# TensorE in program order after the first ninth, and a strided head's second products laid out with the summands adjacent

## The chip, the cores and the metric

One Trainium2 chip, one core, one launch. The metric is the device time of the execution in microseconds (us), the median of the runs shown. Profiles are of one profiled execution each.

## The reference, cut to what matters

Inputs: `q`, `k`, `v` of 8 samples x 8 heads x 576 positions x 64, and the weights `U` (576 x 32), `V` (32 x 576), `w_ch1` (512 x 2048), `w_ch2` (2048 x 512).

```python
scores = q @ k.T / 8                                  # per sample and head, 576 x 576
mask_local   = (rel >= 0) & (rel < 32)                # heads 0 to 3, rel = i - j
mask_strided = (rel >= 0) & (j % 32 == i % 32)        # heads 4 to 7
attn = softmax(where(mask, scores, -1e9)) ; x = attn @ v      # x: 8 x 576 x 512
u  = x + (x.T @ U @ V).T                              # mix along the positions, rank 32
ch = relu(u @ w_ch1) @ w_ch2
out = u + ch
```

## The kernel before, in words

**The large products.** The 8 x 576 = 4608 rows of `u` are worked off in nine blocks of 512 columns (`n` = 0 to 8; here: ninths 0 to 8). Eight of them are the first 512 positions of a sample; the last ninth is the 64 remaining positions of all eight. A ninth has 16 slices `fc` of the 2048 hidden features. `gemm1(n, fc)` (L598) makes one slice in PSUM (`ph`, two buffers) with 12 matmuls of 128x128 by 128x512; ScalarE makes `gh` (Relu) from it, VectorE `gl`, the remainder of the rounding, in `gemm1_out` (L615). `gemm2(n, fc)` (L625) adds that slice to the four accumulators with 12 more matmuls. `gemm2` lags two slices behind (`LAG`). The two `acc` tiles take the whole pool, so the first `gemm2` of a ninth needs the accumulators that `finish` (L656) of the ninth before empties: VectorE adds `ul`, GpSimd adds `uh`, a DMA stores `o`.

**The loop and its ticks.** In the loop over `n` at L916 each slice is cut into four pieces of 6 matmuls, and after each piece comes a `tick` (L814): 64 ticks in a ninth, each with 6 large matmuls. A tick takes one step of each task that is due. While ninth `n` is multiplied, `plan(n)` (L800) brings sample `b = n + 1` to its `u`: `pairs` (the four local heads as two pairs, `attention_pair`, L318, staggered by `run_staggered`, L667), `mix0` and `mix1` (`mix_t`, L462: x times U for the local and for the strided half), `u0` and `u1` (`u_local`, L512; `u_strided`, L528; `u_tail`, L578: times V, plus x, split into two parts). The number after the name is the first tick, a name in brackets the task that must have been written before.

**The strided heads.** `strided_heads(b)` (L348) works the four strided heads of a sample without TensorE: a residue class of 18 positions per partition, `st0` holding q and later the result, `st1` holding k and then v. GpSimd multiplies q by 9 keys at a time into `tmp` (L366), VectorE adds over the 64 dimensions into `s_st`; softmax; then GpSimd multiplies the 18 weights of a row by v into `tmp` (L392; 27 products a sample, of 64 to 576 elements a partition), and VectorE adds over the positions `j` into `st0`. In `tmp` the order is (j, d), so that VectorE reads with a step of 64 or 32 elements. VectorE then transposes the result into `xS`, and ScalarE copies it into `x_str`, which `mix1` reads. In all 74 calls of the generator, at 1.3 a tick (1.45 for the first sample that takes this way). They begin in the last ticks of the ninth before (`EARLY`, L933).

**What sets the order.** `InOrder` (L59) ties each instruction of an engine to the one traced before it, as long as the class's `on` is true. It is switched off for all engines at the end of ninth 0 (L912). From then on the framework's scheduler orders each engine's queue by a timeline of its own, with the traced order as priority. Each engine then works its queue strictly in that order: an instruction that waits holds up everything behind it. The same holds for the DMA queue of SyncE.

**The small products of TensorE** (`px`) share one PSUM tile: one may begin only when the readers of the one before are through. `mix_steps` (L422) takes four partial sums over U in PSUM, copies the first into SBUF (`ta`) and adds the other three there with VectorE. `ta` lies in unused rows of `x_loc` or `x_str` (rows 64 to 95 of the last slot).

The pool `att` has seven buffers for everything short-lived: kT, qT, s_sb, blocks, PT, tmp, xT, xS, tl and o.

Of the kernel before, what the change touches and what calls it, by code (L numbers as in the profile page):

```python
# [14 lines left out]
ALU = mybir.AluOpType  # L15
AX = mybir.AxisListType
# [8 lines left out]
NB = B * S // TB  # L25
NSP = 2
LAG = 2
EARLY = 56


ATT_BUFS = 7
# [16 lines left out]
def fused_kernel(ctx, tc, lqk, lv, eqk, ev, sqkv, U, V, wts, masks, eye, out):  # L48
# [10 lines left out]
    class InOrder:  # L59
# [5 lines left out]
        def __getattr__(self, name):  # L65
            op = getattr(self.engine, name)

            def call(*args, **kwargs):
                with tc.issue_after(self.last) if InOrder.on and self.last is not None else nullcontext():
                    r = op(*args, **kwargs)  # L70
                self.last = r.ins
                return r

            return call
# [243 lines left out]
    def attention_pair(b, pr, loaded=None):  # L318
        if loaded is None:
            loaded = pair_loads(b, pr)  # L320
            for _ in range(3):
                yield
        kT, qT, vt = loaded
        sp = masked(kT, qT)
        yield
        s_sb = masked_shifted(sp, masks_sb[:, 0:320])
        yield
        exponentials(s_sb)
        yield
        yield  # L330
        turned(s_sb.rearrange("p t h (e x) -> p t (h e) x", x=32), p_store[pr])
        yield
        yield
        PT = fetched(p_store[pr], "PT")
        for _ in range(6 + 9 * pr):
            yield
        op = outputs(PT, vt, lambda c: 160 * (c % 4) + 32 * (c // 4))
        yield
        normalised(op, pr)
        yield  # L340
        turned(x_loc[:, :, 128 * pr:128 * pr + 128].rearrange("p t (e x) -> p t e x", x=32), x_store[pr])
        yield

    o_str = {}

    def strided_heads(b):  # L348
        st = [ap_.tile([128, NCH * D], F32, name=f"st{x}") for x in range(2)]
        sq, sk = (z.rearrange("p (i d) -> p i d", d=D) for z in st)  # L350
        for x in range(2):
            dma(out=st[x], in_=sqkv[b - NSP, x])
        yield
        s_st = ap_.tile([128, NCH, NCH], F32, name="s_st")
        nc.gpsimd.memset(s_st, 8.0 * NEG)
        late = []

        def flush(n):
            while len(late) > n:
                late.pop(0)()  # L360

        for i in range(NCH):
            for j0 in range(0, i + 1, 9):
                n = min(9, i + 1 - j0)
                tmp = att([128, 9, D], "tmp")
                nc.gpsimd.tensor_tensor(out=tmp[:, 0:n], in0=sk[:, j0:j0 + n], in1=sq[:, i:i + 1].broadcast_to([128, n, D]),  # L366
                                        op=ALU.mult)
                late.append(lambda tmp=tmp, n=n, i=i, j0=j0: vector.tensor_reduce(
                    out=s_st[:, i, j0:j0 + n], in_=tmp[:, 0:n], axis=AX.X, op=ALU.add))
                flush(1)  # L370
                yield
        flush(0)
        sv = sk
        dma(out=st[1], in_=sqkv[b - NSP, 2])
        yield
        m_st = ap_.tile([128, NCH], F32, name="m_st")
        vector.tensor_reduce(out=m_st, in_=s_st, axis=AX.X, op=ALU.max)
        vector.tensor_tensor(out=s_st, in0=s_st, in1=m_st.broadcast_to([128, NCH, NCH]), op=ALU.subtract)
        scalar.activation(out=s_st, in_=s_st, func=AF.Exp, scale=0.125)
        yield  # L380
        yield
        vector.tensor_reduce(out=m_st, in_=s_st, axis=AX.X, op=ALU.add)
        vector.tensor_scalar(out=m_st, in0=m_st, scalar1=1e-9, scalar2=None, op0=ALU.add)
        vector.reciprocal(out=m_st, in_=m_st)
        vector.tensor_tensor(out=s_st, in0=s_st, in1=m_st.broadcast_to([128, NCH, NCH]), op=ALU.mult)
        yield
        for i in range(NCH):
            step = D if i < 9 else D // 2
            for d0 in range(0, D, step):
                tmp = att([128, (i + 1) * step], "tmp")  # L390
                tv = tmp.rearrange("p (j d) -> p j d", d=step)
                nc.gpsimd.tensor_tensor(out=tv, in0=sv[:, 0:i + 1, d0:d0 + step],  # L392
                                        in1=s_st[:, i, 0:i + 1].broadcast_to([128, i + 1, step]), op=ALU.mult)
                late.append(lambda tv=tv, i=i, d0=d0, step=step: vector.tensor_reduce(
                    out=sq[:, i, d0:d0 + step], in_=tv.rearrange("p j d -> p d j"), axis=AX.X, op=ALU.add))
                flush(1)
                yield
        flush(0)
        yield
        o_str[b] = []  # L400
        for e in range(2):
            xT = att([128, S], "xS")
            vector.transpose(out=xT.rearrange("p (i r) -> p i r", r=32), in_=sq[:, :, 32 * e:32 * e + 32])
            o_str[b].append(xT)
        yield
        for h in range(4):
            rows = slice(32 * h, 32 * h + 32)
            xh = x_str.rearrange("p t (e h x) -> p t h e x", e=2, h=4)[:, :, h]
            oh = sq[rows].rearrange("p i (e x) -> p i e x", e=2)
            for i4 in range(4):  # L410
                scalar.copy(out=xh[32 * i4:32 * i4 + 32, 0:4], in_=oh[:, i4:16:4])
                if i4 % 2:
                    yield
            for i4 in range(2):
                scalar.copy(out=xh[32 * i4:32 * i4 + 32, 4], in_=oh[:, 16 + i4])
            yield
# [5 lines left out]
    def mix_steps(b, half):  # L422
        x, uv = (x_str, 1 if b < NSP else 0) if half else (x_loc, 0)
        ps_a = psx2()[:, 0, 0:256]
        for j in range(4):
            tensor.matmul(ps_a[32 * j:32 * j + 32, :], U_sb[:, uv, j, :], x[:, j, :], start=True, stop=False,
                             skip_group_check=True, tile_position=(0, 32 * j))
        for j in range(4):
            part = slice(64 * j, 64 * j + 64)
            tensor.matmul(ps_a[32 * j:32 * j + 32, part], U_sb[0:64, uv, 4, :], x[0:64, 4, part], start=False, stop=True,  # L430
                             skip_group_check=True, tile_position=(0, 32 * j))
        yield 1
        ta = x[64:96, 4, :]
        scalar.copy(out=ta, in_=ps_a[0:32, :])
        yield 1
        for j in range(1, 4):
            vector.tensor_tensor(out=ta, in0=ps_a[32 * j:32 * j + 32, :], in1=ta, op=ALU.add)
        if b not in tsts:
            tsts[b] = ap_.tile([96, DM], F32R, name="tst")
        yield 1  # L440
        dst = tsts[b][:, 256 * half:256 * half + 256]
        scalar.copy(out=dst[0:32], in_=ta)
        scalar.copy(out=dst[32:64], in_=ta)
        yield 1
        vector.tensor_tensor(out=dst[64:96], in0=ta, in1=dst[0:32].bitcast(F32), op=ALU.subtract)
# [16 lines left out]
    def mix_t(b, half):  # L462
        finished(mix_steps(b, half))
# [114 lines left out]
    def u_tail(b):  # L578
        finished(u_tail_steps(b))
# [87 lines left out]
    def run_staggered(gens, lag):  # L667
        live, waiting, n = [], list(gens), 0
        while live or waiting:
            if waiting and n % lag == 0:  # L670
                live.append(waiting.pop(0))
            n += 1
            for g in list(live):
                if next(g, "end") == "end":
                    live.remove(g)
            yield
# [115 lines left out]
    def task(gen, key, start, rate=1.0, after=()):  # L792
        return [gen, key, start, rate, after, 0.0]

    def calls(*fns):
        for fn in fns:
            fn()
            yield

    def plan(n):  # L800
        b = n + 1
        if b < B:
            return [
                task(run_staggered([attention_pair(b, 0), attention_pair(b, 1)], 8), "pairs", 0, 1.0),
                task(calls(lambda: mix_t(b, 0)), "mix0", 43, 1.0, ("pairs",)),
                task(u_local(b), "u0", 48, 1.0, ("mix0",)),
                task(calls(lambda: mix_t(b, 1)), "mix1", 51 if n == 1 else 49, 1.0, ("str",)),
                task(calls(lambda: u_strided(b), lambda: u_tail(b)), "u1", 54 if n == 1 else 56, 1.0, ("mix1", "u0")),
            ]
        if b == B:  # L810
            return [task(u_rest(), "rest", 12)]
        return []
# [67 lines left out]
    def first_block():  # L880
# [18 lines left out]
        while pieces or agenda:  # L899
# [9 lines left out]
                if delay:  # L909
                    agenda.append((now + delay, item[1], item[2]))  # L910
            clock["now"] += 1
        InOrder.on = False  # L912

    first_block()
    heads = None
# [111 lines left out]
```

## Time and profile before

| | |
|---|---|
| time, median of 3 runs (least to most) | 923.17 us (920.92 to 924.85) |
| the profiled execution | 923.34 us, span 921.6 us |
| TensorE busy | 889.6 us, 97% of the span |
| VectorE busy | 565.3 us, 61% |
| GpSimd busy | 383.4 us, 42% |
| ScalarE busy | 256.6 us, 28% |
| granted TensorE clock | 1.00 throughout |

How to read it: PE is TensorE (its matmuls), DVE VectorE, ACT ScalarE, POOL GpSimd, SP the engine that issues the DMAs. Almost every line is L70, the helper that issues an instruction, so groups are told apart by the tile written and the tiles read (`gl<-ph,gh`). A figure in square brackets is the idle time of the engine just before an instruction, and after the arrow what ended it.

### The profile page before, as it was taken

What the parts mean: (1) busy time and instruction counts of PE and PEld (TensorE: products, weight loads), DVE (VectorE), ACT (ScalarE), POOL (GpSimd) and SP (SyncE); (2) the same over time, 40 slices, a digit from 0 to 9 for tenths busy, and PEclk for the clock granted to TensorE, in tenths of its full rate; (3) what the DMA queues carried; (4) which work ended last, traced back from release to release, by engine and by line L of the source; (5) the groups of instructions that cost most, each with busy time, mean ns of one, the idle gap of its engine ahead of it and who ended that gap; (6) DMA issues with size and microseconds to landing.
All of it is one profiled execution on the core that took longest, in us unless ns stands there. A gap on an engine that the chain in (4) does not pass through costs nothing.

```text
span 921.6 us, 16237 instructions
## 1 busy us (share of the span) xinstructions
PE 889.6 (97%) x6622; PEld 706.0 (77%) x6622; DVE 565.3 (61%) x967; ACT 256.6 (28%) x514; POOL 383.4 (42%) x410
## 2 busy tenths in 40 slices
PE   7999999998999989999999899999999999999998
PEld 4677778876788678877887688867887888888886
DVE  5988875778587855696568756686569431112112
ACT  5866741105110521133112321052114311111110
POOL 1000024764876566475748466557646220002000
PEclk9999999999999999999999999999999999999999
DMA  9992112222143303321142304331331030001001
GB/s 292 405 405 98 53 58 68 77 89 87 32 127 96 99 26 106 96 96 53 48 127 62 109 13 127 96 97 32 101 96 46 1 98 0 1 1 46 1 0 47
DMA packets 46779, 80.95 MB, mean 88 GB/s; under 512 B 10896, under 2 KB 23952, under 8 KB 46704
## 3 DMA queue, kind: packets, MB, share of 16 engines
q1 hardware_dynamic: 46704, 79.91, 26.7%
q8 instruction: 52, 0.85, 0.4%
q14 instruction: 23, 0.19, 0.1%
HBM read 61.54 MB, written 18.35 MB: 87 GB/s over the span
## 4 chain that ended last, share of the span: by engine, by line
PE 45%; DVE 23%; DMA 14%; POOL 10%; issue 3%; SPq 3%; ACT 1%; POOLq 0%; DVEq 0%; ACTq 0%
PE ph L70 21%; PE acc L70 21%; DVE st L70 11%; POOL tmp L366 7%; DMA xd<-blocks 4%; DMA pd<-blocks 3%; PE px L70 3%; SPq L93 3%; DMA st<-in_sqkv_dram 3%; DMA raw<-in_wts_dram 2%; DVE s_st L70 2%; DVE gl L70 2%; POOL tmp L392 2%; DVE blocks L70 2%; DVE x_loc L70 1%
## 5 line engine op out<-in xcount | busy, mean ns | idle before, releaser
L70 PE MATMUL ph<-uh,w 128*128 128x512 f32 x1152 | 385.3, 394 | 11.7 <-DVE gl L70 11.7
L70 PE MATMUL acc<-gh,w 128*128 128x512 f32 x1152 | 382.3, 391 | 0.4 <-DVE o L70 0.4
L70 PEld LDWEIGHTS ph<-uh,w 128*128 128x128 f32 x1152 | 216.0, 188 | 64.1 <-DVE gl L70 17.8
L70 PEld LDWEIGHTS acc<-gh,w 128*128 128x128 f32 x1152 | 216.1, 188 | 46.9 <-DVE o L70 0.8
L366 POOL TENSOR_TENSOR tmp<-st,st 128x576 f32<-128x576 f32 (+6 forms) x162 | 169.6, 1074 | 193.3 <-DVE w L70 116.7
L70 PE MATMUL acc<-gl,w 128*128 128x512 f32 x576 | 224.8, 390 | 0.0
L70 PE MATMUL ph<-ul,w 128*128 128x512 f32 x576 | 224.6, 390 | 0.0
L70 DVE SCALAR_TENSOR_TENSOR gl<-ph,gh 128x512 fp32r<-128x512 f32 x144 | 98.9, 687 | 189.6 <-ACT gh L70 189.1
L70 ACT ACTIVATE gh<-ph 128x512 fp32r<-128x512 f32 x144 | 85.5, 597 | 418.6 <-PE ph L70 407.4
L392 POOL TENSOR_TENSOR tmp<-st,s_st 128x448 f32<-128x448 f32 (+7 forms) x162 | 134.8, 869 | 77.5 <-DMA pd<-blocks 22.9
L70 DVE TENSOR_REDUCE st<-tmp 128x64 f32<-128x64 f32 (+8 forms) x162 | 135.3, 878 | 33.4 <-POOL tmp L392 32.6
L70 DVE TENSOR_REDUCE s_st<-tmp 128x9 f32<-128x576 f32 (+6 forms) x162 | 91.3, 572 | 89.3 <-POOL tmp L366 86.2
L70 PEld LDWEIGHTS acc<-gl,w 128*128 128x128 f32 x576 | 108.1, 188 | 22.2
L70 PEld LDWEIGHTS ph<-ul,w 128*128 128x128 f32 x576 | 108.2, 188 | 21.1
L662 POOL TENSOR_TENSOR o<-o,uh 128x512 f32<-128x512 f32 x32 | 40.8, 1297 | 132.8 <-DVE o L70 132.8
L70 ACT COPY x_str<-st 32x256 f32<-32x256 f32 (+1 forms) x144 | 50.4, 350 | 81.9 <-DVE st L70 80.4
L525 POOL TENSOR_TENSOR ul<-xT,uh 128x512 fp32r<-128x512 f32 x12 | 15.4, 1301 | 37.3 <-ACT uh L70 37.3
L70 ACT ACTIVATE s_sb<-s_sb 128x640 f32<-128x640 f32 x20 | 14.7, 736 | 44.1 <-DVE s_sb L70 44.1
L70 DVE SCALAR_TENSOR_TENSOR raw<-raw 128x512 int32<-128x512 int32 x32 | 22.0, 688 | 3.5 <-ACT raw L70 2.9
L70 DVE SCALAR_TENSOR_TENSOR cv<-cv,raw 128x512 int32<-128x512 int32 x32 | 22.2, 692 | 1.1
L70 DVE TENSOR_TENSOR o<-acc,ul 128x512 f32<-128x512 f32 x32 | 20.7, 686 | 2.8 <-DMA out_dram<-o 2.1
L70 DVE TENSOR_TENSOR w<-cv,w 128x512 fp32r<-128x512 f32 x32 | 21.8, 684 | 0.8 <-ACT w L70 0.7
(124 smaller groups left out, 487.7 us busy)
## 6 DMA issues: line engine op xcount, KB each, us to landing
raw<-in_wts_dram SPq DMA_DIRECT2D x32, 512.0 KB
st<-in_sqkv_dram SPq DMA_DIRECT2D x18, 576.0 KB
out_dram<-o SPq DMA_DIRECT2D x35, 256.0 KB
vt<-in_lv_dram SPq DMA_DIRECT2D x14, 585.0 KB
pd<-blocks SPq DMA_DIRECT2D x48, 80.0 KB
PT<-pd SPq DMA_DIRECT2D x12, 320.0 KB
xd<-blocks SPq DMA_DIRECT2D x48, 80.0 KB
xT<-xd SPq DMA_DIRECT2D x12, 320.0 KB
```

The source lines that it names most:

```text
L70: r = op(*args, **kwargs)
L93: last_dma[0] = nc.sync.dma_start(out=out, in_=in_).ins
L366: nc.gpsimd.tensor_tensor(out=tmp[:, 0:n], in0=sk[:, j0:j0 + n], in1=sq[:, i:i + 1].broadcast_to([128, n, D]), op=ALU.mult)
L392: nc.gpsimd.tensor_tensor(out=tv, in0=sv[:, 0:i + 1, d0:d0 + step], in1=s_st[:, i, 0:i + 1].broadcast_to([128, i + 1, step]), op=ALU.mult)
L525: nc.gpsimd.tensor_tensor(out=ul, in0=src, in1=uh.bitcast(F32), op=ALU.subtract)
L662: nc.gpsimd.tensor_tensor(out=o, in0=o, in1=uh[:, m].bitcast(F32), op=ALU.add)
```

## The change

From ninth 1 on, TensorE alone keeps to the traced order; the other engines are still ordered by the scheduler. GpSimd writes the second products of the strided heads as (d, j), and VectorE reads them in sequence. The sums over U of the strided half (`ta` of `mix1`) are kept in the first 32 partitions of `st1` in place of `x_str`. The rest is ticks: the second pair of local heads begins to load 4 ticks after the first (before 8) and computes its scores at tick 13 (before 11); the first pair's outputs come at tick 20 (before 15), the second's at 34 (before 32); `mix0` at 42, `u0` at 50, `mix1` at 50, `u1` at 57 with an empty step between `u_strided` and `u_tail`; the strided heads of the next sample begin two ticks later (`EARLY` 58).

```diff
-EARLY = 56
+EARLY = 58
...
-                with tc.issue_after(self.last) if InOrder.on and self.last is not None else nullcontext():
+                with tc.issue_after(self.last) if self.on and self.last is not None else nullcontext():
...
-            for _ in range(3):
+            for _ in range(3 + 6 * pr):
                 yield
...
-        for _ in range(6 + 9 * pr):
+        for _ in range(11 + 4 * pr):
             yield
...
-    o_str = {}
+    o_str, sums_in = {}, {}
...
                 tmp = att([128, (i + 1) * step], "tmp")
-                tv = tmp.rearrange("p (j d) -> p j d", d=step)
-                nc.gpsimd.tensor_tensor(out=tv, in0=sv[:, 0:i + 1, d0:d0 + step],
+                tv = tmp.rearrange("p (d j) -> p d j", d=step)
+                nc.gpsimd.tensor_tensor(out=tv.rearrange("p d j -> p j d"), in0=sv[:, 0:i + 1, d0:d0 + step],
                                         in1=s_st[:, i, 0:i + 1].broadcast_to([128, i + 1, step]), op=ALU.mult)
                 late.append(lambda tv=tv, i=i, d0=d0, step=step: vector.tensor_reduce(
-                    out=sq[:, i, d0:d0 + step], in_=tv.rearrange("p j d -> p d j"), axis=AX.X, op=ALU.add))
+                    out=sq[:, i, d0:d0 + step], in_=tv, axis=AX.X, op=ALU.add))
...
-        o_str[b] = []
+        o_str[b], sums_in[b] = [], st[1][0:32, 0:256]
...
-        ta = x[64:96, 4, :]
+        ta = sums_in[b] if half and b in sums_in else x[64:96, 4, :]
         scalar.copy(out=ta, in_=ps_a[0:32, :])
...
-                task(run_staggered([attention_pair(b, 0), attention_pair(b, 1)], 8), "pairs", 0, 1.0),
-                task(calls(lambda: mix_t(b, 0)), "mix0", 43, 1.0, ("pairs",)),
-                task(u_local(b), "u0", 48, 1.0, ("mix0",)),
-                task(calls(lambda: mix_t(b, 1)), "mix1", 51 if n == 1 else 49, 1.0, ("str",)),
-                task(calls(lambda: u_strided(b), lambda: u_tail(b)), "u1", 54 if n == 1 else 56, 1.0, ("mix1", "u0")),
+                task(run_staggered([attention_pair(b, 0), attention_pair(b, 1)], 4), "pairs", 0, 1.0),
+                task(calls(lambda: mix_t(b, 0)), "mix0", 42, 1.0, ("pairs",)),
+                task(u_local(b), "u0", 50, 1.0, ("mix0",)),
+                task(calls(lambda: mix_t(b, 1)), "mix1", 50, 1.0, ("str",)),
+                task(calls(lambda: u_strided(b), lambda: None, lambda: u_tail(b)), "u1", 57, 1.0, ("mix1", "u0")),
...
-        InOrder.on = False
+        InOrder.on, tensor.on = False, True
```

## The prediction

> **What bounds the kernel now.** I read the page first, then busy time by ninth (the stretches view), then who made TensorE wait.
>
> ```profile
> span 921.6 us, 16237 instructions
> ...
> PE 889.6 (97%) x6622; PEld 706.0 (77%) x6622; DVE 565.3 (61%) x967; ACT 256.6 (28%) x514; POOL 383.4 (42%) x410
> ```
>
> ```profile
> 139.53:240.32 100.79, 96.10 (x710) 75.86 (x708) 70.94 (x119) 22.76 (x51) 61.65 (x66) 1.00 0.25 79
> 240.32:342.74 102.42, 96.67 (x718) 76.83 (x717) 73.68 (x126) 25.61 (x55) 67.38 (x70) 1.00 0.27 79
> 342.74:441.44 98.70, 95.77 (x714) 76.37 (x712) 69.93 (x121) 24.27 (x53) 60.88 (x66) 1.00 0.27 82
> 441.44:540.56 99.12, 95.89 (x714) 76.45 (x714) 69.93 (x121) 24.27 (x53) 61.22 (x66) 1.00 0.27 82
> 540.56:639.89 99.33, 95.94 (x714) 76.45 (x714) 69.85 (x121) 24.28 (x53) 61.16 (x66) 1.00 0.27 82
> 639.89:737.17 97.28, 95.78 (x715) 76.62 (x715) 64.39 (x111) 24.27 (x53) 49.15 (x51) 1.00 0.20 59
> 737.17:824.21 87.04, 87.04 (x386) 72.07 (x385) 16.12 (x24) 11.76 (x20) 5.06 (x4) 1.00 0.09 26
> ```
>
> Columns: stretch, its length, then busy time of PE, PEld, DVE, ACT, POOL. The stretches are ninths 1 to 7, each from its first `gemm1` matmul to the next ninth's. Ninth 7 prepares no sample and is the pure rate: 87.04 us for 384 large matmuls, 0.227 each, 1.36 a tick. The six before it carry about 9 us of small products, and TensorE is idle in them for length minus busy: 4.69, 5.75, 2.93, 3.23, 3.39, 1.50, together **21.5 us**. That is all that order and waits can give back; the rest is matmuls. Ninth 0 isn't touched, and ninths 7 and 8 hold no step that moves. TensorE's own waits (us in total, times, longest) say what the idle time is:
>
> ```profile
> PE ph L70 <- DVE gl L70: 11.7, 13, 1.7
> PE px L70 <- DVE x_str L70: 7.4, 4, 2.7
> ...
> PE px L70 <- DVE xT L70: 2.1, 1, 2.1
> ...
> PE px L70 <- DVE tst L70: 0.3, 1, 0.3
> ```
>
> Both large ones end on VectorE, though VectorE is busy only 70 of 99 us. In its timeline of ninth 3:
>
> ```profile
> 408.68 4.33 DVE L70 TENSOR_REDUCE st<-tmp 128x32 f32<-128x512 f32 x4
> 414.84 0.68 DVE L70 SCALAR_TENSOR_TENSOR gl<-ph,gh 128x512 fp32r<-128x512 f32 x1
> 424.81 0.62 DVE L70 TENSOR_REDUCE s_st<-tmp 128x7 f32<-128x448 f32 x1 [0.56 <-POOL tmp L366]
> 426.06 0.42 DVE L70 TENSOR_TENSOR x_str<-px,x_str 32x256 f32<-32x256 f32 x1
> ```
>
> First, `gl` sits behind a run of second-product reductions, and TensorE, which needs `ph` emptied, waits. Second, `mix1`'s sums (`x_str<-px`) sit behind first-product reductions of the next sample that are themselves waiting for GpSimd, and the next small product waits for their PSUM tile.
>
> **The reductions laid out in sequence.** The rows by shape:
>
> ```profile
> L70 DVE TENSOR_REDUCE st<-tmp 128x32 f32<-128x576 f32 x12 | 14.4, 1196 | 0.0
> L70 DVE TENSOR_REDUCE s_st<-tmp 128x9 f32<-128x576 f32 x66 | 49.5, 752 | 55.0 <-POOL tmp L366 54.6
> L70 DVE TENSOR_REDUCE s_st<-tmp 128x1 f32<-128x64 f32 x12 | 2.6, 216 | 11.4 <-POOL tmp L366 9.0 <-POOL s_st L355 2.4
> L70 DVE TENSOR_REDUCE st<-tmp 128x64 f32<-128x64 f32 (+8 forms) x162 | 135.3, 878 | 33.4 <-POOL tmp L392 32.6
> ```
>
> 576 elements cost 1196 ns with a step and 752 in sequence. The two sequential rows give 1.047 ns an element and 149 ns a call. A sample has 27 second reductions over 10,944 elements in all: 27 x 0.149 + 10.944 x 1.047 = 15.5 us, against 135.3 / 6 = 22.6. **VectorE gains 7.1 us a ninth**, all in the run that holds up `gl`; what remains of that run is under POOL's pace (next row), so reductions no longer pile up. I take the 11.7 us of `gl` waits as gone. If DVE's cover fails, they stay: that is the price.
>
> **The products written with a step.** GpSimd now writes 4-byte elements 8 to 72 bytes apart. No row shows that on GpSimd. The nearest is ScalarE's `uh<-px`, the only other write with a step, against the same size written in sequence:
>
> ```profile
> L392 POOL TENSOR_TENSOR tmp<-st,s_st 128x576 f32<-128x576 f32 x18 | 20.6, 1157 | 0.0
> L70 ACT CAST uh<-px 128x512 fp32r<-128x512 f32 x4 | 3.9, 987 | 0.9 <-PE px L70 0.9
> L70 ACT ACTIVATE gh<-ph 128x512 fp32r<-128x512 f32 x144 | 85.5, 597 | 418.6 <-PE ph L70 407.4 <-PE acc L70 6.0 <-DVE s_st L70 4.8
> L392 POOL TENSOR_TENSOR tmp<-st,s_st 128x448 f32<-128x448 f32 (+7 forms) x162 | 134.8, 869 | 77.5 <-DMA pd<-blocks 22.9
> ```
>
> ScalarE pays (987 - 597) / 512 = 0.76 ns an element more, and ends at 1.93 ns an element. GpSimd already takes 1157 / 576 = 2.0. If the step limits the pace, it hides under GpSimd's own: 0. If it adds, 10.944 x 0.76 = 8.3 us a sample on 134.8 / 6 = 22.5. A gain is excluded: the number of elements and the reads stay. I take **+2 us a sample**, near the hidden end, because GpSimd is already slower per element than the stepped write of ScalarE.
>
> [...]
>
> **The sums over U in `st1`.** This frees `mix1`'s sums from waiting behind the next sample: k can be loaded into `st1` only when the sums are through, so no reduction of the next sample can stand before them. The `x_str` and `xT` waits go, 7.4 + 2.1 + 0.3 us. The price is that the next strided heads start later. They are a loop of their own, and its rows for one turn, from the chain of waits and the timelines, with the group of the first products, are:
>
> ```profile
> 319.17 6.42 POOL tmp L366 x8
> 370.97 2.83 POOL L366 TENSOR_TENSOR tmp<-st,st 128x576 f32<-128x576 f32 x2
> 379.03 1.69 POOL L392 TENSOR_TENSOR tmp<-st,s_st 128x64 f32<-128x64 f32 x4 [5.24 <-DVE rt L70]
> 389.41 20.08 POOL L392 TENSOR_TENSOR tmp<-st,s_st 128x384 f32<-128x384 f32 x22 [3.25 <-DMA xd<-blocks]
> 414.96 1.01 ACT L70 COPY x_str<-st 32x64 f32<-32x64 f32 x4 [1.53 <-DVE st L70]
> 419.84 7.58 POOL L366 TENSOR_TENSOR tmp<-st,st 128x64 f32<-128x64 f32 x9 [9.92 <-DMA st<-in_sqkv_dram]
> L366 POOL TENSOR_TENSOR tmp<-st,st 128x576 f32<-128x576 f32 (+6 forms) x162 | 169.6, 1074 | 193.3 <-DVE w L70 116.7
> ```
>
> First products 319.17 to 373.80, 54.6 us; softmax to 379.03, 5.2; second products to 409.49, 30.5; reductions and copies to 415.97, 6.5; the load of q to 419.84, 3.9: 100.7. So this loop turns once a ninth with little slack, and most of it is waiting: GpSimd's own work is 169.6 / 6 = 28.3 us in the first stage and 22.5 in the second.
>
> After the change a turn has: `mix1` and its sums, about 5 us (estimate: its matmuls, one copy, three sums, two casts and a difference, each 0.4 to 0.9, and a `gl` between); the load, 3.6 (as q's now); first products 37 to 52 us (GpSimd's own 28.3 with 8 to 9 of other work in its queue, up to today's 54.6 less the two `ul` that now come before); softmax 5.2; second products 24.5 to 32.5; the tail 3.5, since the last reductions no longer queue. Together **79 to 102 us**, with the middle at 90, against the 95.8 that TensorE needs in a ninth anyway. Where it is longer, TensorE in order pays all of the excess at `mix1`, because nothing may pass it. I put 1.0 us a ninth on ninths 2 to 6 for turns in the upper part: 5 us.
>
> **Ninth 1** starts from nothing, so no earlier turn helps it.
>
> ```profile
> 192.15 22.53 POOL L392 TENSOR_TENSOR tmp<-st,s_st 128x64 f32<-128x64 f32 x27 [11.79 <-DMA st<-in_sqkv_dram]
> 221.67 1.02 ACT L70 COPY x_str<-st 32x64 f32<-32x64 f32 x4 [2.09 <-DVE st L70]
> 348.28 0.97 PE L70 MATMUL px<-kT,qT 64*32 64x64 f32 x72
> 349.18 0.50 PE L70 MATMUL ph<-uh,w 128*128 128x512 f32 x1
> ```
>
> The second products end at 214.68, and `x_str` 8 us later. With 2 us more for GpSimd and 3.5 for the tail, `x_str` is complete at 220.2, 80.7 after the ninth's start. `mix1` stands at tick 52 there (74 calls at 1.45 end at tick 51): 52 x 1.36 plus five small products of about 1.1 (0.90 from 348.28 to 349.18, and slower neighbours) is 76.2. **TensorE waits 4.5 us**, about what it idles there now. In the other ninths `mix1` stands at tick 51, at 74.9.
>
> **TensorE in order, elsewhere.** The other small products lie a few ticks behind their inputs: `mix0` at 42 after the second pair is normalised at 35, `u0`'s product at 54, `u_strided` at 57, `u_tail` at 59, with 2.7 us and more between, against 1.3 to 2 us for the readers of the PSUM tile. The accumulators have gemm1 of slice 2 (2.7 us) and half a `gemm2` as cover for two adds of 0.69. The scores at 13 need a load issued at tick 4, 12 us earlier. I count 0.5 us for these over all, hidden by those ticks; a missed one would cost 1 to 2 us a ninth.
>
> **The sum.** 923.3 (profiled; its span and 1.7 around it, and the median is 923.2, so both stand for the same) - 21.5 + 4.5 + 5 + 0.5 = 911.8, rounded to **912 us**.
>
> **Rivals.** *No change, about 922 us, 0.18*: the waits only move. If the strided loop keeps today's waits (a turn of 99 to 102 us), each ninth is as long as before and TensorE idles at `mix1` in place of at `gl` and `u0`. For it: the loop is 100.7 us now and its start is put later by the sums; against: 4 to 5 us of the tail was reductions queueing. *Slower, about 938 us, 0.20*: GpSimd's stepped write adds its 0.76 ns or more. A turn with 6.3 us more than I took is 85 to 108; at 101 to 102, ninths 2 to 6 take about 510 against 496.9 now, and ninth 1 waits 10.8 in place of 4.5, less its 4.7: 923.3 + 13 + 1.5 to 6. It decides from a second product of about 1.1 us on the mean (869 ns now) if the waits stay in the upper half. For it: the stepped rows of both other engines; against: GpSimd's pace is already that of a stepped access. [...] *That the order isn't kept* would show as no wait at `mix1`; VectorE's gain alone then gives about 912 too, so it needs no price of its own.
>
> **How the numbers follow.** My forecast of a clear gain has 0.62. Half a per cent, 4.6 us, is about what a measurement of this kernel can tell from no change, so faster means under 918.6 and slower over 927.8. The forecast's own range is 901 (all waits gone, none new) to 918; with the even case whole and the near half of the slower one it is 901 to 930. Faster 0.62, same 0.18, slower 0.20.
>
> **What would show it.** Right: second reductions of 576 elements near 752 ns; second products under 1.25 us at 576; waits of `ph` for `gl` under 3 us in all; no wait of `u0`'s product for the sums; what waits remain stand at `mix1` for ScalarE's copies into `x_str`, the longest in ninth 1. Wrong: second products over 1.5 us; ninths of 99 us or more with one long wait at `mix1`; long waits at the pairs' small products for loads of kT or PT, which I have set at nearly nothing.

## The result and the profile after

896.52 us (median of 4 runs, 894.98 to 898.91) against 924.01 us for the kernel before (4 runs, 920.92 to 926.21): ratio 0.9707, 95% interval 0.9671 to 0.9744. That is 27 us faster, where 912 was forecast with a range of 901 to 930. The profiled execution took 898.91 us, its span is 897.1. Of the four runs of the kernel with the old ticks below, one was slow (1136.31 us, granted clock 0.74) and is left out of its figure.

The stretches view of the changed kernel, ninths 1 to 7 (length, then busy time of PE, PEld, DVE, ACT, POOL):

```profile
140.84:237.28 96.44, 95.67 (x713) 76.55 (x712) 63.37 (x122) 24.39 (x53) 62.24 (x66) 1.00 0.26 78
237.28:332.37 95.09, 95.09 (x713) 76.74 (x712) 62.57 (x122) 24.37 (x53) 61.29 (x66) 1.00 0.28 85
332.37:427.44 95.07, 95.07 (x713) 76.74 (x712) 62.84 (x121) 24.51 (x53) 60.69 (x65) 1.00 0.28 85
427.44:522.51 95.07, 95.07 (x713) 76.76 (x712) 62.89 (x122) 24.50 (x53) 62.13 (x66) 1.00 0.28 86
522.51:617.59 95.09, 95.09 (x713) 76.73 (x712) 62.78 (x122) 24.49 (x53) 61.86 (x67) 1.00 0.28 85
617.59:712.71 95.11, 95.11 (x713) 76.74 (x712) 60.11 (x114) 24.50 (x53) 54.90 (x56) 1.00 0.21 64
712.71:799.75 87.04, 87.04 (x385) 72.10 (x384) 16.14 (x24) 11.76 (x20) 5.06 (x4) 1.00 0.07 22
```

In ninths 2 to 6 length and busy time are the same: TensorE shows no idle time. Only ninth 1 keeps 0.77 us. Against before (597.64 us for the six ninths) they take 571.87: **25.8 us less**; between the spans it is 24.5, since ninth 1 began 1.3 us later here (ninth 0 has two stretches, 7.35 to 10.70 and 21.00 to 24.40, at a granted clock of 0.50). VectorE has 4 to 11 us less work a ninth (418.7 to 374.6 in the six), GpSimd no less (361.4 and 363.1). The waits of TensorE that carried the argument are gone from the list; what is left of `ph` for `gl` is one wait in ninth 1:

```profile
PE ph L70 <- DVE gl L70: 0.8, 1, 0.8
```

The groups behind the two priced steps, by shape:

```profile
L392 POOL TENSOR_TENSOR tmp<-st,s_st 128x576 f32<-128x576 f32 x18 | 22.3, 1289 | 0.0
...
L70 DVE TENSOR_REDUCE st<-tmp 128x32 f32<-128x576 f32 x12 | 8.7, 727 | 0.0
```

```profile
L392 POOL TENSOR_TENSOR tmp<-st,s_st 128x448 f32<-128x448 f32 (+7 forms) x162 | 136.7, 943 | 54.5 <-DVE s_st L70 31.3
```

The reduction of 576 elements fell from 1196 to 727 ns, and the record of the product that now writes with a step rose from 1157 to 1289. The last row, from the page, takes all second products together: the mean record grew from 869 to 943 ns, but their busy time, in which overlapping records count once, only from 134.8 to 136.7 us.

One turn of the strided heads, from the timelines of GpSimd, ScalarE, TensorE and the DMA queue in ninth 3:

```profile
321.07 0.75 POOL L366 TENSOR_TENSOR tmp<-st,st 128x64 f32<-128x64 f32 x2 [17.25 <-DMA st<-in_sqkv_dram]
362.21 2.83 POOL L366 TENSOR_TENSOR tmp<-st,st 128x576 f32<-128x576 f32 x2
371.31 1.73 POOL L392 TENSOR_TENSOR tmp<-st,s_st 128x64 f32<-128x64 f32 x4 [6.27 <-DVE s_st L70]
381.72 15.03 POOL L392 TENSOR_TENSOR tmp<-st,s_st 128x352 f32<-128x352 f32 x16 [1.47 <-DMA xd<-blocks]
417.02 0.75 POOL L366 TENSOR_TENSOR tmp<-st,st 128x64 f32<-128x64 f32 x2 [19.84 <-DMA st<-in_sqkv_dram]
```

```profile
398.08 1.01 ACT L70 COPY x_str<-st 32x64 f32<-32x64 f32 x4 [0.61 <-DVE st L70]
```

```profile
408.76 0.89 PE L70 MATMUL px<-x_str,U_sb 128*32 128x256 f32 x16
```

```profile
412.46 0.34 SPq L93 DMA_DIRECT2D st<-in_sqkv_dram  x1
```

`x_str` is complete at 399.09 and `mix1` begins at 408.76: **9.67 us of slack** on the step that the prediction charged. `mix1` and its sums take 3.7 us to the load of k at 412.46, the load 4.6, and the first product of the next sample stands at 417.02, 95.95 us after that of the turn before (321.07). A turn is busy for 95.95 - 9.67 = 86.3 us.

### The profile page after: what moved, and what is told of

It reads as the page before. It is cut to its first block, busy times and chain, and to the rows that moved or that the text cites. A ratio compares the mean times of both kernels' runs of the same rounds, so it can differ in the third digit from the quotient of the medians.

```text
span 897.1 us, 16253 instructions
## 1 busy us (share of the span) xinstructions
PE 883.7 (99%) x6622; PEld 707.8 (79%) x6622; DVE 520.9 (58%) x967; ACT 257.7 (29%) x514; POOL 384.7 (43%) x410
## 4 chain that ended last, share of the span: by engine, by line
PE 75%; DVE 0%; ACT 0%; DVEq 0%; issue 0%
PE acc L70 36%; PE ph L70 35%; PE px L70 4%; DVE gl L70 0%; ACT gh L70 0%; DVE o L70 0%; DVEq L1021 0%
## 5 line engine op out<-in xcount | busy, mean ns | idle before, releaser
L392 POOL TENSOR_TENSOR tmp<-st,s_st 128x448 f32<-128x448 f32 (+7 forms) x162 | 136.7, 943 | 54.5 <-DVE s_st L70 31.3
L70 DVE TENSOR_REDUCE st<-tmp 128x64 f32<-128x64 f32 (+8 forms) x162 | 90.1, 567 | 40.9 <-POOL tmp L392 40.1
L525 POOL TENSOR_TENSOR ul<-xT,uh 128x512 fp32r<-128x512 f32 x12 | 15.5, 1299 | 32.0 <-ACT uh L70 32.0
```

What stands on the lines that cost most here:

```text
L392: nc.gpsimd.tensor_tensor(out=tv.rearrange("p d j -> p j d"), in0=sv[:, 0:i + 1, d0:d0 + step], in1=s_st[:, i, 0:i + 1].broadcast_to([128, ...
L525: nc.gpsimd.tensor_tensor(out=ul, in0=src, in1=uh.bitcast(F32), op=ALU.subtract)
```

## The experiments

Two short names help: *layout* is the (d, j) order, *order* TensorE in program order. The kernels below were measured in three groups, each with 7 runs of the kernel before beside it (medians 924.5 us each), so ratios are given; a time is the median of 4 runs (old ticks: of 3), and figures of ninths, waits and rows are from the profiled execution.

| kernel | order | layout | sums | ticks | us | ratio (95%) |
|---|---|---|---|---|---|---|
| changed | x | x | x | x | 896.52 | 0.9707 (0.9671 to 0.9744) |
| without order | | x | x | x | 899.95 | 0.9744 (0.9721 to 0.9766) |
| without layout | x | | x | x | 905.72 | 0.9805 (0.9773 to 0.9837) |
| without sums in st1 | x | x | | x | 898.63 | 0.9740 (0.9708 to 0.9772) |
| old ticks | x | x | x | | 952.05 | 1.0318 (1.0285 to 1.0350) |
| layout alone | | x | | | 905.38 | 0.9794 (0.9755 to 0.9832) |
| layout and sums | | x | x | | 901.81 | 0.9762 (0.9743 to 0.9781) |
| ticks alone | | | | x | 906.65 | 0.9810 (0.9787 to 0.9832) |
| layout and ticks | | x | | x | 897.98 | 0.9726 (0.9704 to 0.9747) |

### Undoing one part of the change

**Without order.**

```diff
...
-        InOrder.on, tensor.on = False, True
+        InOrder.on = False
```

> The changed kernel with TensorE left to the scheduler after ninth 0; layout, sums in st1 and ticks stay changed. Theory Q (VectorE's queue: the waits were made by second-product reductions ahead of gl, and by mix1's sums held behind the next sample's reductions; the order of TensorE itself is worth little): 897 to 902 us. Rival O (the order is the gain: the scheduler puts small products where their inputs are late): 912 us or more, with waits of 2 to 4 us a ninth at the small products.

899.95 us. Theory Q holds: the order itself is worth about 3 us, and by the intervals, which overlap, not surely that. The stretches show where such a difference can lie: ninths 4 to 6 are 95.52 us each where they are 95.07 to 95.11 in order, without any idle time.

```profile
427.10:522.62 95.52, 95.52 (x713) 76.67 (x712) 62.13 (x121) 24.32 (x53) 62.46 (x67) 1.00 0.28 85
```

The timeline of that ninth shows why: the scheduler cuts the second pair's scores in two (6 records, then 66 about 24 large matmuls later), so one more run of large matmuls is broken; large ones beside a small product start 0.32 to 0.34 us apart in place of 0.227.

```profile
442.43 0.31 PE L70 MATMUL px<-kT,qT 64*32 64x64 f32 x6
448.35 0.88 PE L70 MATMUL px<-kT,qT 64*32 64x64 f32 x66
```

**Without layout.** Product and reduction as before.

```diff
-                tv = tmp.rearrange("p (d j) -> p d j", d=step)
-                nc.gpsimd.tensor_tensor(out=tv.rearrange("p d j -> p j d"), in0=sv[:, 0:i + 1, d0:d0 + step],
+                tv = tmp.rearrange("p (j d) -> p j d", d=step)
+                nc.gpsimd.tensor_tensor(out=tv, in0=sv[:, 0:i + 1, d0:d0 + step],
...
-                    out=sq[:, i, d0:d0 + step], in_=tv, axis=AX.X, op=ALU.add))
+                    out=sq[:, i, d0:d0 + step], in_=tv.rearrange("p j d -> p d j"), axis=AX.X, op=ALU.add))
```

> The changed kernel with the second products written as (j, d) again and read with a step. Theory Q: the 11.7 us of waits of ph for gl come back, about 908 us, second reductions at 1196 ns for 576 elements again. Rival O: 897 to 902 us, since order, sums and ticks stay.

905.72 us, 9 more, near what Theory Q said. The waits for `gl` come back, but not all of them (6.0 us where 11.7 were before). That the new ticks put the long run of reductions elsewhere against the `gl` that TensorE needs would explain it, and was not looked into.

```profile
PE ph L70 <- DVE gl L70: 6.0, 7, 1.7
PE px L70 <- DVE x_loc L70: 2.6, 3, 1.5
```

**Without the sums in `st1`.**

```diff
...
-        ta = sums_in[b] if half and b in sums_in else x[64:96, 4, :]
+        ta = x[64:96, 4, :]
```

> The changed kernel with mix1's sums in x_str again. Theory Q: the next sample's reductions stand before mix1's sums again, 1.5 to 2 us a ninth at u0's or u1's product, about 906 us. Rival O: 897 to 902 us.

898.63 us, 2 us more, with intervals that overlap. Here Theory Q missed by 7 us and the time of rival O came out: ninths 2 to 6 are 95.04 us each, and the only wait for the sums is one of 2.1 us in ninth 1. The wait for the sums behind other reductions needs no `st1` to go away; see the run with EARLY alone.

**Old ticks.** The whole plan of before, with `EARLY = 56` and the pairs' steps between load, scores and outputs as before.

```diff
...
-                task(run_staggered([attention_pair(b, 0), attention_pair(b, 1)], 4), "pairs", 0, 1.0),
+                task(run_staggered([attention_pair(b, 0), attention_pair(b, 1)], 8), "pairs", 0, 1.0),
...
-                task(u_local(b), "u0", 50, 1.0, ("mix0",)),
-                task(calls(lambda: mix_t(b, 1)), "mix1", 50, 1.0, ("str",)),
-                task(calls(lambda: u_strided(b), lambda: None, lambda: u_tail(b)), "u1", 57, 1.0, ("mix1", "u0")),
+                task(u_local(b), "u0", 48, 1.0, ("mix0",)),
+                task(calls(lambda: mix_t(b, 1)), "mix1", 51 if n == 1 else 49, 1.0, ("str",)),
+                task(calls(lambda: u_strided(b), lambda: u_tail(b)), "u1", 54 if n == 1 else 56, 1.0, ("mix1", "u0")),
```

> The changed kernel with the ticks of before (pairs 8 apart, outputs at 15 and 32, mix0 43, u0 48, mix1 49, u1 56 without an empty step, EARLY 56). With TensorE in order a small product that stands before its inputs stops everything. Theory Q: the scores and outputs of the pairs wait 1 to 2 us a ninth, 903 to 910 us. A third theory T (the ticks are the larger part, order alone would lose): 920 us or more.

952.05 us: slower than before, as theory T said. The run with the old pairs below shows the wait.

### One or two parts on the kernel of before

Each takes hunks of the change as they stand. The layout alone:

```diff
-                tv = tmp.rearrange("p (j d) -> p j d", d=step)
-                nc.gpsimd.tensor_tensor(out=tv, in0=sv[:, 0:i + 1, d0:d0 + step],
+                tv = tmp.rearrange("p (d j) -> p d j", d=step)
+                nc.gpsimd.tensor_tensor(out=tv.rearrange("p d j -> p j d"), in0=sv[:, 0:i + 1, d0:d0 + step],
...
-                    out=sq[:, i, d0:d0 + step], in_=tv.rearrange("p j d -> p d j"), axis=AX.X, op=ALU.add))
+                    out=sq[:, i, d0:d0 + step], in_=tv, axis=AX.X, op=ALU.add))
```

> The kernel of before with the second products laid out (d, j), nothing else. Theory Q (VectorE's queue made the waits): the waits of ph for gl go, those of the small products for mix1's sums stay, 910 to 914 us. Rival T (the ticks carry most of the gain): 919 us or more.

905.38 us, better than either theory: the layout alone gives 19 of the 27 us (15.5 to 22.7 by the interval). Its waits of TensorE:

```profile
PE px L70 <- DVE x_str L70: 6.7, 4, 1.8
...
PE px L70 <- DVE xT L70: 1.4, 1, 1.4
...
PE ph L70 <- DVE gl L70: 0.8, 2, 0.5
```

`gl` falls from 11.7 to 0.8, the waits for the sums stay at 6.7. So the layout acts on the wait that the prediction named, and takes more than its idle time with it: in the six ninths the idle time is 12.3 us less than before (9.2 for 21.5), the ninths together 14.9 us shorter.

The layout and, besides it, the sums in `st1`:

```diff
...
-        ta = x[64:96, 4, :]
+        ta = sums_in[b] if half and b in sums_in else x[64:96, 4, :]
```

> The kernel of before with the layout and the sums in st1; scheduler's order and ticks of before. Theory Q: both kinds of wait go, 900 to 905 us. Rival T: 915 us or more, since the ticks stay and TensorE is held at other places (a turn of the strided heads starts later by the sums).

901.81 us, as Theory Q said: with the layout, the sums in `st1` give 3.6 us, and ninths 3 to 6 are 95.04. In its ninth 2 one wait of 4.2 us stays, ahead of the second pair's outputs, which the profile puts down to nothing; that ninth takes 102.19 us.

All the ticks, and nothing else:

```diff
-EARLY = 56
+EARLY = 58
...
-            for _ in range(3):
+            for _ in range(3 + 6 * pr):
...
-        for _ in range(6 + 9 * pr):
+        for _ in range(11 + 4 * pr):
...
-                task(u_local(b), "u0", 48, 1.0, ("mix0",)),
+                task(u_local(b), "u0", 50, 1.0, ("mix0",)),
```

(and the other rows of the plan as in the change).

> The kernel of before with the new ticks, scheduler's order, old layout, sums in x_str. Theory Q: 918 to 925 us, the waits on VectorE are where they were. Rival T: 905 to 912 us.

906.65 us, rival T: 18 us, with neither layout nor order nor `st1`. No wait for `mix1`'s sums is left in its list, and `gl` is halved:

```profile
PE ph L70 <- DVE gl L70: 5.3, 7, 1.6
...
PE px L70 <- DVE x_loc L70: 1.4, 3, 0.6
```

The same ticks together with the layout's hunk:

```diff
-                tv = tmp.rearrange("p (j d) -> p j d", d=step)
+                tv = tmp.rearrange("p (d j) -> p d j", d=step)
...
-EARLY = 56
+EARLY = 58
```

> Layout and ticks, without the order and without the sums in st1. Theory Q: 907 to 912 us (the waits for mix1's sums stay). Rival T: about 900 us, like the kernel without the order alone.

897.98 us, as Rival T said, with an interval that overlaps that of the whole change. So layout and ticks together give the gain within the noise, and what the order and `st1` add to them isn't told apart from nothing. Layout (19) and ticks (18) do not add to 37: each removes a large part of the same 26 us.

### EARLY alone, the old pairs, and GpSimd slowed down

```diff
-EARLY = 56
+EARLY = 58
```

> The kernel of before with EARLY at 58 alone, so that the next sample's strided heads are traced two ticks later. Theory E (this number alone takes the next sample's reductions out from in front of mix1's sums): the waits for x_str go, 7 to 10 us, about 915 us. Rival P (the moved pairs made the gain of the ticks): 921 us or more.

915.61 us, ratio 0.9914 (0.9891 to 0.9936): Theory E. The waits of the small products for `x_str` leave the list, `gl` stays as it was:

```profile
PE ph L70 <- DVE gl L70: 11.0, 10, 2.3
...
PE px L70 <- DVE xT L70: 2.3, 1, 2.3
```

VectorE's timeline in ninth 3 of that kernel:

```profile
422.70 1.34 DVE L70 TENSOR_TENSOR x_str<-px,x_str 32x256 f32<-32x256 f32 x3
431.66 0.62 DVE L70 TENSOR_REDUCE s_st<-tmp 128x7 f32<-128x448 f32 x1 [1.93 <-POOL tmp L366]
```

In the prediction's rows of before, the reduction to 128x7 stands at 424.81, ahead of the sums at 426.06. So two ticks later in the traced order are enough for the scheduler to put `mix1`'s sums ahead of the longer reductions of the next sample (six short ones still come before them); the sums in `st1` put them ahead of all. The other half of what the ticks give (906.65) lies with the moved pairs, `mix0`, `u0` and `u1`, and wasn't split further.

The old pairs within the changed kernel (the rest of the ticks new):

```diff
-            for _ in range(3 + 6 * pr):
+            for _ in range(3):
...
-        for _ in range(11 + 4 * pr):
+        for _ in range(6 + 9 * pr):
...
-                task(run_staggered([attention_pair(b, 0), attention_pair(b, 1)], 4), "pairs", 0, 1.0),
+                task(run_staggered([attention_pair(b, 0), attention_pair(b, 1)], 8), "pairs", 0, 1.0),
```

> The changed kernel with the ticks of the two pairs as before (8 apart, 3 steps from load to scores, outputs after 6 and 15). Theory K (TensorE in order stands at the second pair's scores until kT and qT are loaded, since the load waits for a buffer behind the four o tiles): about 950 us as with all old ticks, waits of px for a load of 5 to 10 us a ninth. Rival: the loss lies with EARLY, mix0, u0 and u1, then 905 us or less.

939.82 us, ratio 1.0176 (1.0152 to 1.0199): 43 of the 56 us that the old ticks cost. Theory K has the place right and the size too high by 10 us; the other ticks cost the remaining 12. The list, and the timelines of ninth 3 (344.64 to 447.21), TensorE and the DMA queue:

```profile
PE px L70 <- DMA qT<-in_lqk_dram: 36.9, 6, 7.0
```

```profile
350.17 0.97 PE L70 MATMUL px<-kT,qT 64*32 64x64 f32 x72
368.40 1.32 PE L70 MATMUL px<-kT,qT 64*32 64x64 f32 x72 [6.16 <-DMA qT<-in_lqk_dram]
```

```profile
361.58 0.44 SPq L93 DMA_DIRECT2D out_dram<-o  x1
362.12 0.38 SPq L93 DMA_DIRECT2D kT<-in_lqk_dram  x1
362.71 1.15 SPq L93 DMA_DIRECT2D out_dram<-o  x1
363.95 0.46 SPq L93 DMA_DIRECT2D qT<-in_lqk_dram  x1
```

TensorE stands at the second pair's scores in each of the six ninths, and in this one the queue issues kT and qT only between the stores of `o`. In the changed kernel the queue issues that kT at 334.54, 2.2 us after the ninth begins, and the scores at 352.65 find it there. Left to the scheduler (layout and sums, 901.81) the old ticks leave ninths 3 to 6 at 95.04 us: in its ninth 3 the second pair's scores stand 26.2 us after the start (361.39), where TensorE in order came to them after 17.6 and waited to 23.8. That the buffers of `o` are what holds the load was not tried by itself.

A memset ahead of each second product, of half of `tmp`:

```diff
+                nc.gpsimd.memset(tmp[:, 0:(i + 1) * step // 2], 0.0)
                 nc.gpsimd.tensor_tensor(out=tv.rearrange("p d j -> p j d"), in0=sv[:, 0:i + 1, d0:d0 + step],
```

> The changed kernel with a memset of half of tmp ahead of each second product on GpSimd: 27 of about 0.09 us and 5,472 elements of 0.84 ns, about 7 us a sample. Theory S (a turn of the strided heads is 85 us, and mix1 stands 9.7 us behind x_str in ninths 2 to 6, 4.5 in ninth 1): only ninth 1 pays, 2 to 3 us, 897 to 901 us. Rival L (the turn has no slack, and the gain hangs on GpSimd's pace): 7 us a ninth, about 935 us.

900.27 us, ratio 0.9740 (0.9717 to 0.9763): Theory S. The memsets took 41.1 us in all, 6.9 a sample, and ninths 3 to 6 stay at 95.17 to 95.57 (ninth 2 takes 96.15, with a wait of 0.7 for `gl`). ScalarE's last copy into `x_str` and `mix1` in that kernel, ninth 3:

```profile
406.21 1.02 ACT L70 COPY x_str<-st 32x64 f32<-32x64 f32 x4 [1.93 <-DVE st L70]
```

```profile
410.27 0.89 PE L70 MATMUL px<-x_str,U_sb 128*32 128x256 f32 x16
```

Of 9.67 us of slack 3.0 are left (407.23 to 410.27): the 6.9 us went into it. Ninth 1 takes 2.3 us more (98.73 against 96.44), as Theory S had it, but not at `mix1`: its 2.2 us of idle time are three waits of `ph` for `gl`. There the 4.5 us of slack are used up, with the last copies into `x_str` ending at 220.83 and `mix1` beginning at 220.11.

Two memsets of the whole of `tmp`:

```diff
+                for _ in range(2):
+                    nc.gpsimd.memset(tmp, 0.0)
```

> As the run with 7 us, but two memsets of the whole of tmp, about 23 us a sample. Theory S: the slack is used up, 13 us in each of ninths 2 to 6 and 18 in ninth 1, about 980 us, with the waits at mix1's first matmuls for ScalarE's copies into x_str. Rival W (GpSimd's waits for buffers and loads shrink with it): 940 us or less.

984.76 us, ratio 1.0659 (1.0634 to 1.0685): Theory S again, near its 980. The memsets take 21.9 us a sample, more than the slack, TensorE stops at `mix1`, and a ninth is 109 to 113 us:

```profile
PE px L70 <- ACT x_str L70: 62.8, 12, 6.9
```

## Why the prediction was wrong, point by point

The direction and the cause were right: TensorE waited on VectorE's queue, and the reductions in sequence cost VectorE 15.0 us a sample (90.1 / 6) where 15.5 was predicted. The range was missed for two terms, both mis-sized in the same direction: the new waits at `mix1` and the ceiling of what could be regained.

**The waits at `mix1`, "TensorE in order pays all of the excess": charged 4.5 + 5 us, and 0.5 for other new waits; measured 0 at `mix1`, and one wait of 0.8 for `gl`.** The turn of the strided heads was put at 79 to 102 us with the middle at 90. It is 86.3, with 9.7 us of slack, and the runs with slowed products show that slack directly: in ninths 3 to 6, 6.9 us more a sample vanish in it but for 0.5 us at most, and 21.9 do not. Within the turn I had kept half of GpSimd's waits: first products 44.0 us (321.07 to 365.04) where I had 37 to 52, second products 25.4 where I had 24.5 to 32.5, and the copies 2.3 after them where I had 3.5. For ninth 1 the rows are:

```profile
187.29 2.44 POOL L392 TENSOR_TENSOR tmp<-st,s_st 128x64 f32<-128x64 f32 x5 [6.92 <-DMA st<-in_sqkv_dram]
214.39 1.02 ACT L70 COPY x_str<-st 32x64 f32<-32x64 f32 x4 [1.93 <-DVE st L70]
219.93 0.89 PE L70 MATMUL px<-x_str,U_sb 128*32 128x256 f32 x16
```

`x_str` was complete 74.6 us after the start and not 80.7, mostly because the second products began 46.5 us after it and not 52.6 as before; and `mix1` stood at 79.1 and not at 76.2. A tick comes after its piece, so every place in my list was 1.36 us early.

**The ceiling, "all that order and waits can give back": 21.5 us, measured 25.8, with 0.8 of idle time still left in it.** I took length minus busy time. A wait costs more than the idle time it shows. The wait of ninth 3 in the timeline of before:

```profile
401.43 0.39 PE L70 MATMUL acc<-gh,w 128*128 128x512 f32 x1
402.56 0.50 PE L70 MATMUL ph<-uh,w 128*128 128x512 f32 x1 [0.75 <-DVE gl L70]
402.90 0.40 PE L70 MATMUL ph<-ul,w 128*128 128x512 f32 x1
```

From start to start it is 1.13 and 0.34 us where the run has 0.227 each: 1.0 us lost for 0.75 shown. The busy column of a ninth with waits (95.77) is therefore no floor; without them it is 95.07. Over the six ninths the busy time fell by 5.1 us (576.2 to 571.1). With 21.5 + 5.1 in place of the ceiling and 0.8 in place of the 10 us of new waits my own sum gives 923.3 - 26.6 + 0.8 = 897.5; the profiled run, whose ninth 0 was 1.3 us longer, took 898.9. These are measured terms, so this closes the account and tests nothing.

**The stepped write: charged 2.0 us a sample, measured 0.3.** The 2.0 seems met if the records are read, which are 74 ns longer on the mean (27 x 0.074 = 2.0); but they overlap the next product, and GpSimd's busy time grew by (136.7 - 134.8) / 6 = 0.3 us a sample. Products of 544 elements follow each other after 1065 ns before and 1067 in the changed kernel, though their records grew from 1106 to 1183. So the step is nearly hidden, as the prediction's lower end said. ScalarE's 987 ns, from which the other end was worked out, is a mean over three records with a step of 1.09 to 1.15 us and one without of 0.59, so it was no price of a step either.

**Attribution.** The prediction gave the `gl` waits to the layout and those for the sums to `st1`. Layout alone does end the `gl` waits (0.8 left). The waits for the sums also end by EARLY alone (915.61), which the prediction did not price; undoing `st1` in the full change costs 2 us, within the noise. The order was taken as neutral, which is near (about 3 us). But "a missed one would cost 1 to 2 us a ninth", of the ticks, was low: with the old ticks and the order it is 56 us, 9 a ninth. The rival of no order ("about 912") was 899.95, nearly as far off as the forecast.

**Rivals.** "Slower" needed 6.3 us more of GpSimd a sample than the forecast took, and its busy time grew by 0.3 in all. Its point of decision, a mean of 1.1 us, was too low: with 6.9 us more a sample the kernel is still 24 us faster than before, and only with 21.9 is it slower. Of the signs named, the reductions of 576 elements (727 ns) and the waits for `gl` (0.8 us) came out; the products of 576 at 1289 ns did not stay under 1.25 us, and the one wait that remained was not at `mix1`.

## What to carry to other kernels

Find the slack of the step that a reordered engine will wait at by slowing its input on purpose: two runs bracket it, here between 6.9 us, which it took up, and 21.9, which it did not. An engine put in strict order gains little here (about 3 us) and stakes everything on the places of its inputs; move the loads first. Take the floor of a stage, and the price of an instruction, from start-to-start times: busy time held 5.1 us that went with the waits, and a mean record of 74 ns more hid that GpSimd's pace had hardly changed.

## What the runs showed of the hardware that had not been expected

Around some of TensorE's waits its granted clock falls to half. In the kernel with the old pairs the wait of 6.16 us ends at 368.40, and the stretches around it read (length, PE busy, granted clock, DMA):

```profile
355.00:362.00 7.00, 7.00 (x32) 1.00 0.26 90
362.00:368.40 6.40, 0.25 (x2) 0.72 0.80 258
368.40:371.00 2.60, 2.60 (x75) 0.50 0.04 12
371.00:374.00 3.00, 3.00 (x13) 0.89 0.00 0
```

In the 2.6 us after the wait the clock is 0.50, and waits of 6.15 us on the mean (36.9 / 6) cost 7.0 to 7.5 us a ninth (102.1 to 103.6 against 95.1 to 96.4); the mean clock is 0.97 in each of the six. Shorter waits have a low stretch behind them too: with EARLY alone a wait of 2.30 us ends at 399.35, and the clock is 0.50 from 399.80 to 403.19; with the layout alone one of 1.85 us ends at 417.26, and it is 0.50 from 417.40 to 420.80. Both low stretches last 3.4 us, and the ninth that each lies in has a mean clock of 0.98. The length of a wait does not decide alone: in the kernel before, TensorE waited 2.73 us up to 329.20 at a clock of 1.00, and it is 1.00 from there to 336.00.

A write with a step made GpSimd's records longer (1157 to 1289 ns at 576 elements) and hardly its pace (1.9 us of busy time more over 162 products).
